# Cos-GLU behind an FFT filter: the first product of the last 18 token chunks by seven block products instead of eight, and the two small chunks moved forward

## The chip, the core and the metric

One NeuronCore of a Trainium2 chip runs the whole program. The metric is the device time of one execution in microseconds, lower is better. Before the change it is 2460.77 us, the median of three runs (2459.45 to 2461.38).

## What is computed

```python
batch, seq, dim = (8, 3008, 256)
X = np.fft.rfft(x, axis=1)
Y = X * (filt_r + 1j * filt_i)[None]
y = np.fft.irfft(Y, n=seq, axis=1)          # float32
x = y.reshape(24064, 256)                    # tokens
h = x @ w_in                                 # 256 x 2048
g = h * np.cos(h)
out = g @ w_out                              # 2048 x 256, float32
```

## The kernel before

**Staging.** The filter runs as a two-factor FFT (47 x 64) in four stages on TensorE, batch by batch, with intermediate results in DRAM. Its last step, `stage4` (L500 to L546), leaves the tokens of a chunk in SBUF as two rounded parts, `yh` (high) and `yl` (low remainder). The two dense products follow chunk by chunk: 50 chunks of 470 tokens (5 groups of 94) and, at the end, 2 of 282 (`_chunks`).

**A step.** A chunk has 8 steps `s`, each of 256 of the 2048 hidden columns. `hidden(c, s)` is the first product: for two halves `u` of 128 hidden columns and two halves `t` of the 256 inputs, three matmuls (weights high x tokens high, high x low, low x high), so 12 matmuls of 128x128 weights against 470 tokens into two PSUM banks `hp` (L561). `gate` (L569 to L584) then makes h*cos(h) from PSUM: a rounding on ACT (L571), a subtraction on DVE (L572), the sine on ACT (L575), a multiplication on DVE (L576), a rounded copy `gh` on ACT (L581) and the remainder `gl` on GpSimd (L582), each over 128x940. `project(c, s)` is the second product, 12 matmuls (L596) that add onto two banks `acc0`, `acc1`; after the eighth step ACT scales them (L605) and its queue sends them out.

**Order.** The program's PE order is written out: step k issues `hidden` of step k, then `project` of step k-2 (LAG). So a gate has the time of four blocks of 12 matmuls. Between the blocks `run_due` puts the pieces of the FFT of later batches by a list of due times, in slots, 64 to a chunk; `stage4` of a chunk stands there too. On ACT, DVE and GpSimd the order comes from the compiler's list of what is ready. In PSUM `ps_f` has 2 banks for the FFT, `ps_h` 4 (two `hp`), `ps_o` 2.

**Lines.** L528 is `stage4`'s matmul, L537 its copy on ACT, L538 and L539 its sums on DVE, L542 and L543 the split of its result; L261 to L263 are three matmuls of an FFT stage, L340 an FFT copy from PSUM on DVE, L380 an FFT product on DVE with one PSUM input, L639 and L642 a fill and a copy on GpSimd at the start.

Of the kernel before, what the change touches and what calls it, by code (L numbers as in the profile page):

```python
# [22 lines left out]
NJ = NB // 2  # L23
TJ = 2 * NA
# [138 lines left out]
def fft_filter_then_cos_glu(ctx: ExitStack, tc: tile.TileContext, ins, outT):  # L163
# [339 lines left out]
    def stage4(c, half):  # L503


        j0, n = chunks[c]
        r, w = n * NK, n * Q
        rows = z2.rearrange("j q d -> (j q) d")[j0 * 2 * Q + half * w :][:w]
        zf = fft.tile([P, 2, D], F32, name="z4", tag="ld", bufs=5)[:r]
        if c == 0:  # L510
            zf = zf[: 10 * (n23 - DIRECT)]
            of = z2c[2 * half : 2 * half + 2].rearrange("a g i (k d) -> (g i k) a d", k=2)
            load = nc.sync.dma_start(zf, of)
            hold[:] = [load.ins]
# [19 lines left out]
        y = fft.tile([P, NDT, 5, NA], F32, name="y4", bufs=1)[:, :, :n]  # L534
# [11 lines left out]
        done.add((c, half))  # L546


    gs, accs, first_gate = {}, {}, []

# [16 lines left out]
            gs[c, s] = gate(hp[:, :, :nt], nt, nc.vector if c == 0 else nc.gpsimd)  # L567

    def gate(h, nt, engine):  # L569
        g = moe.tile([P, 2, 5 * TJ], F32, name="g")[:, :, :nt]  # L570
# [8 lines left out]
        gh = moe.tile([P, 2, 5 * TJ], F32R, name="gh")[:, :, :nt]  # L579
        gl = moe.tile([P, 2, 5 * TJ], F32R, name="gl")[:, :, :nt]  # L580
        cast = nc.scalar.copy(gh, g)  # L581
        lower = engine.tensor_tensor(gl, g, gh.bitcast(F32), ALU.subtract)  # L582
        hold[1:] = [cast.ins, mult.ins, lower.ins]
        return gh, gl  # L584

    def project(c, s):
        nt = chunks[c][1] * TJ
        if s == 0:
            accs[c] = [ps_o.tile([P, 512], F32, name=f"acc{e}") for e in range(2)]
        gh, gl = gs.pop((c, s))  # L590
        for e in range(2):
            acc = accs[c][e][:, :nt]
            es = slice(e * P, (e + 1) * P)
            for u in range(2):
                for n, (w, g) in enumerate(((0, gh), (1, gh), (0, gl))):
                    nc.tensor.matmul(acc, w_out[s][w][:, u, es], g[:, u],  # L596
                                     start=(s == 0 and u == 0 and n == 0),
                                     stop=(s == NFT // 2 - 1 and u == 1 and n == 2))
                if e == 0 or u == 0:
                    yield  # L600
        if s == NFT // 2 - 1:
            t0 = chunks[c][0] * TJ
            for e in range(2):
                o = moe.tile([P, 5 * TJ], F32, name="o", bufs=2)[:, :nt]
                nc.scalar.activation(o, accs[c][e][:, :nt], AF.Copy, scale=TWO_PI)  # L605
                nc.scalar.dma_start(outT[e * P : (e + 1) * P, t0 : t0 + nt], o)
            del accs[c], ys[c]


    def pipeline(items, parts, gap=2):  # L610

# [81 lines left out]
    def convert(g=None, behind=None):  # L693
        with tc.issue_after((behind or hold)[1]), tc.issue_after((behind or hold)[2]):
            if g is None:
                g = prep.pop(0)(None)
                next(g)
            next(g, None)
# [59 lines left out]
    for c in range(1, len(chunks)):  # L758
        j0, n = chunks[c]
        each = EACH4 if c > 2 else 2 * SLOTS  # L760
        for half in range(2):
            at = [max(SLOTS * NS * c + (2 * half + t) * each - BEFORE4, SLOTS * (3 + 2 * half + t)) for t in range(NDT)]
            b = (2 * j0 + (half + 1) * n - 1) // NB
            plan(stage4(c, half), at[0] - AHEAD4, at, lambda b=b: len(wrote2.get(b, ())) == n23)
    due.sort(key=lambda d: d[0])
    for k in range(len(steps) + LAG):
        parts = []
        if k == 2:
            for g in soon[2:]:
# [75 lines left out]
```

## Time and profile before

| | us |
|---|---|
| median of 3 runs | 2460.77 |
| the profiled execution, device time | 2459.8 |
| its span, first to last instruction | 2457.7 |
| PE busy in the span | 2428.6 |
| GpSimd, ACT, DVE busy | 1606.9, 1616.3, 1442.9 |

The profile is of one execution. A busy PE is not a PE at its peak: a matmul's record runs past the start of the next, so the pace is read from starts (or from the chain, whose pieces don't overlap), not from the records' lengths. The span falls into three stretches: the first batch's FFT and filling up to some 70 us, the steps with the FFT of the other batches between them up to about 1640 us, and the steps alone after that.

### The profile page before, as it was taken

To read this page: it belongs to the slowest core of one execution; us is meant where nothing else is said; L and a number is where in the kernel's file an instruction comes from. 1 tells how busy PE (TensorE), PEld (TensorE's weight loads), DVE (VectorE), ACT (ScalarE), POOL (GpSimd) and SP (SyncE) were. 2 spreads that over 40 slices of the span, in tenths; PEclk is the share of its full clock that TensorE was granted. 3 is DMA by queue.
4 is the path that set the end of the run, shared out by engine and by line. 5 is a ranking of instruction groups with operands and counts; after the bars stand their busy time and mean duration, and the time that the engine had idled before them with its cause. 6 is when DMAs were issued, how large, how long until landed. Compare 5 with 4: busy or idle time off the path is not lost.

```text
span 2457.7 us, 32775 instructions
## 1 busy us (share of the span) xinstructions
PE 2428.6 (99%) x11671; PEld 2105.6 (86%) x11671; DVE 1442.9 (59%) x1814; ACT 1616.3 (66%) x2116; POOL 1606.9 (65%) x992
## 2 busy tenths in 40 slices
PE   7999999999999999999999999999999999999999
PEld 2788888888888888888888888888888888888888
DVE  5846756676676667567667766754444444444444
ACT  4866676677676767766776676666556565655665
POOL 3736677878787787878878887844444454444444
PEclk9999999999999999999999999999999999999999
DMA  8932354545554554454446444510000000000000
GB/s 293 270 115 89 107 147 130 178 137 162 150 157 131 148 177 150 131 174 151 142 134 190 148 137 136 165 62 21 28 17 32 17 29 20 21 25 13 17 8 18
DMA packets 185114, 268.98 MB, mean 109 GB/s; under 512 B 19089, under 2 KB 103249, under 8 KB 184953
## 3 DMA queue, kind: packets, MB, share of 16 engines
q1 hardware_dynamic: 151992, 214.72, 29.7%
q10 hardware_dynamic: 32960, 52.18, 5.9%
q8 instruction: 93, 1.52, 0.3%
q14 instruction: 69, 0.56, 0.1%
HBM read 172.96 MB, written 93.86 MB: 109 GB/s over the span
## 4 chain that ended last, share of the span: by engine, by line
PE 94%; DMA 2%; DVE 2%; issue 1%; ACT 1%; POOL 1%; SPq 0%; POOLq 0%; ACTq 0%; DVEq 0%
PE hp L561 42%; PE acc L596 41%; PE ps L528 3%; PE ps L338 2%; PE ps L261 2%; PE ps L262 2%; PE ps L263 2%; DMA ff<-in_fa 1%; PE hp L434 0%; PE ps L311 0%; DVE g L572 0%; DVE sw L379 0%; DVE g L576 0%; DMA raw<-in_w_out 0%; DMA ff<-in_fb 0%
## 5 line engine op out<-in xcount | busy, mean ns | idle before, releaser
L582 POOL TENSOR_TENSOR gl<-g,gh 128x940 fp32r<-128x940 f32 (+1 forms) x408 | 894.4, 2192 | 644.5 <-ACT gh L581 509.7
L561 PE MATMUL hp<-y,w_in 128*128 128x470 f32 (+1 forms) x4992 | 1154.0, 375 | 5.7 <-DVE g L576 5.3
L561 PEld LDWEIGHTS hp<-y,w_in 128*128 128x128 f32 x4992 | 929.5, 189 | 137.6 <-issue 5.9
L596 PE MATMUL acc<-gh,w_out 128*128 128x470 f32 (+1 forms) x3328 | 927.4, 374 | 0.8 <-ACT gh L581 0.5
L572 DVE TENSOR_TENSOR g<-g,hp 128x940 f32<-128x940 int32 (+1 forms) x416 | 464.4, 1116 | 425.6 <-ACT g L571 421.2
L596 PEld LDWEIGHTS acc<-gh,w_out 128*128 128x128 f32 x3328 | 618.7, 189 | 86.6 <-issue 1.5
L576 DVE TENSOR_TENSOR g<-g,hp 128x940 f32<-128x940 f32 (+1 forms) x416 | 464.6, 1117 | 349.4 <-ACT g L575 348.2
L575 ACT ACTIVATE g<-g,half_pi 128x940 f32<-128x940 f32 (+1 forms) x416 | 445.3, 1070 | 236.4 <-DVE g L572 230.0
L596 PE MATMUL acc<-gl,w_out 128*128 128x470 f32 (+1 forms) x1664 | 567.8, 375 | 1.4 <-POOL gl L582 1.4
L571 ACT ACTIVATE g<-hp 128x940 int32<-128x940 f32 (+1 forms) x416 | 391.7, 942 | 235.1 <-PE hp L561 225.5
L581 ACT CAST gh<-g 128x940 fp32r<-128x940 f32 (+1 forms) x416 | 400.6, 963 | 197.4 <-DVE g L576 191.7
L596 PEld LDWEIGHTS acc<-gl,w_out 128*128 128x128 f32 x1664 | 311.9, 188 | 44.7 <-POOL gl L582 2.2
L333 POOL TENSOR_TENSOR xh<-xf,xh 48x512 fp32r<-48x512 f32 x192 | 245.3, 1291 | 42.2 <-ACT xh L332 32.7
L379 DVE SCALAR_TENSOR_TENSOR sw<-ps,sg,f 64x256 f32<-64x256 f32 x336 | 162.4, 483 | 54.0 <-PE ps L263 48.8
L340 DVE COPY z1t<-ps 96x512 f32<-96x512 f32 x192 | 129.4, 684 | 98.6 <-PE ps L338 95.8
L543 POOL TENSOR_TENSOR y<-y,y 128x470 fp32r<-128x470 f32 (+1 forms) x100 | 114.7, 1147 | 48.1 <-ACT y L542 48.0
L332 ACT CAST xh<-xf 96x512 fp32r<-96x512 f32 x192 | 114.8, 618 | 34.3 <-PE ps L338 30.7
L385 POOL TENSOR_TENSOR yl<-ya,yh 128x512 fp32r<-128x512 f32 x84 | 109.0, 1299 | 34.7 <-ACT yh L384 34.2
L528 PEld LDWEIGHTS ps<-m,z 120*128 120x128 f32 (+1 forms) x816 | 114.5, 191 | 9.4 <-issue 0.8
L528 PE MATMUL ps<-m,z 120*128 120x120 f32 (+1 forms) x816 | 114.2, 273 | 0.1
L369 POOL TENSOR_TENSOR zl<-zf,zh 128x512 fp32r<-128x512 f32 x84 | 108.9, 1300 | 6.4 <-ACT zh L368 6.4
L364 POOL TENSOR_TENSOR zf<-zf,zg 128x512 f32<-128x512 f32 x72 | 93.6, 1300 | 13.2 <-DMA zg<-z 12.9
(96 smaller groups left out, 1196.4 us busy)
## 6 DMA issues: line engine op xcount, KB each, us to landing
xf<-in_x SPq DMA_DIRECT2D x224, 192.0 KB
z<-z1t SPq DMA_DIRECT2D x192, 192.0 KB
z<-z SPq DMA_DIRECT2D x98, 240.0 KB
out_t<-o ACTq DMA_DIRECT2D x100, 235.0 KB
f<-in_fb SPq DMA_DIRECT2D x84, 256.0 KB
f<-in_fa SPq DMA_DIRECT2D x84, 256.0 KB
zf<-z SPq DMA_DIRECT2D x84, 256.0 KB
z<-z2t ACTq DMA_DIRECT2D x84, 256.0 KB
```

Of the source, the lines that this page charges most:

```text
L333: nc.gpsimd.tensor_tensor(xh[:Q], xf[:Q, v], xh[:Q].bitcast(F32), ALU.subtract)
L340: nc.vector.tensor_copy(z, ps[: 2 * Q])
L379: nc.vector.scalar_tensor_tensor(sw[to, ks], ps[of, ks], sg[of, kc : kc + 1], fbt[of, ks], ALU.mult, ALU.mult)
L528: mm = nc.tensor.matmul(v[:, t, a * r : (a + 1) * r], zf[:, a, t * P : (t + 1) * P], m, start=c > 0, stop=c > 0 or a == 1)
L561: mm = nc.tensor.matmul(hp[:, u, :nt], w_in[s][w][:, t, fs], y[:, t, :nt], start=(t == 0 and n == 0), stop=(t == NDT - 1 and n == 2))
L571: rounded = nc.scalar.activation(g.bitcast(I32), h, AF.Copy, bias=0.25)
L572: rest = nc.vector.tensor_tensor(g, g.bitcast(I32), h, ALU.subtract)
L575: sine = nc.scalar.activation(g, g, AF.Sin, bias=half_pi, scale=-TWO_PI)
L576: mult = nc.vector.tensor_tensor(g, g, h, ALU.mult)
L581: cast = nc.scalar.copy(gh, g)
L582: lower = engine.tensor_tensor(gl, g, gh.bitcast(F32), ALU.subtract)
L596: nc.tensor.matmul(acc, w_out[s][w][:, u, es], g[:, u], start=(s == 0 and u == 0 and n == 0), stop=(s == NFT // 2 - 1 and u == 1 and n == 2))
```

## The change

The small chunks of 282 tokens become chunks 4 and 5, in place of the last two; the due times are counted in token groups. From chunk 34 (`FAST`) on, a chunk's first product goes by Winograd's form of Strassen's scheme. The operands of a 256-column step are taken as 2x2 blocks: the weights by `t` and `u`, the tokens by `t` and the two halves of the chunk (235 tokens, held as 236). Seven block products replace eight. Four sums of weight blocks (`add_weights`, S1 to S4) are made once, and four of token blocks (T1 to T4) for each chunk in `blocks`, on GpSimd, which takes the place of the end of `stage4`; each is split into a high part and a remainder.

A `quad` handles two steps at once: `product` issues 6 matmuls of 236 columns (3 for each of the two steps) for each of the seven products, 42 in all, into the four banks x (two in turn), v and w of the new pool `ps_q`, and into one bank of `ps_f` for y. Three banks are copied out on ACT between the products that add onto them, and three sums are made on DVE. `factor` does the first four operations of the gate on each of the four results (128x472); the rounded copy goes to GpSimd for two of them and to ACT for the other two, the remainders to GpSimd. `project_quad` is the second product, 24 matmuls a quad with 472 columns. PE's order is again written out: a quad's projection runs one and two quads later. The core of the diff:

```diff
+SMALL, FAST = 4, 34
+HALF = 236
+SUMS, EACH_SUM = 2010, 12
+AHEAD_FAST = (64, 60, 52, 48)
+AFTER_FAST = (3, 7, 11, 15, 19)
...
-    sizes = [5] * ((B * NJ - 6) // 5) + [3, 3]
+    sizes = [5] * SMALL + [3, 3] + [5] * ((B * NJ - 6) // 5 - SMALL)
...
-    ps_h = ctx.enter_context(tc.tile_pool(name="ps_h", bufs=2, space=bass.MemoryType.PSUM))
     ps_o = ctx.enter_context(tc.tile_pool(name="ps_o", bufs=1, space=bass.MemoryType.PSUM))
+    until = ctx.enter_context(ExitStack())
+    ps_h = until.enter_context(tc.tile_pool(name="ps_h", bufs=2, space=bass.MemoryType.PSUM))
...
+        if c >= FAST:
+            e = v.rearrange("p t (i g n) -> p t i g n", g=2, n=NK)
+            yield from blocks(c, half, e)
+            done.add((c, half))
+            return
...
+    def add_weights(s):
+
+        hi, lo = (w.bitcast(F32).rearrange("p t f -> p (t f)") for w in w_in[s])
+        whole = fft.tile([P, 512], F32, name="whole", tag="ld", bufs=5)
+        nc.vector.tensor_tensor(whole, hi, lo, ALU.add)
...
+        nc.vector.tensor_tensor(both[:, 0], a21, a22, ALU.add)
+        nc.vector.tensor_tensor(both[:, 2], a21, a11, ALU.subtract)
+        nc.vector.tensor_tensor(both[:, 1], both[:, 0], a11, ALU.subtract)
+        nc.vector.tensor_tensor(both[:, 3], a12, both[:, 1], ALU.subtract)
...
+        nc.scalar.copy(sums[s][0], both)
+        nc.gpsimd.tensor_tensor(sums[s][1], both, sums[s][0].bitcast(F32), ALU.subtract)
+        yield
...
+    def split(hi, lo, of, cast=nc.scalar.copy):
+        cast(hi, of)
+        nc.gpsimd.tensor_tensor(lo, of, hi.bitcast(F32), ALU.subtract)
...
+        hi, lo = ys[c][:2]
+        yield
+        if half == 0:
+            split(hi[:, :2], lo[:, :2], blk[:, 1:3], nc.vector.tensor_copy)
+            return
...
+        first = fft.tile([P, 2, HALF], F32, name="dif", tag="y4", bufs=1)
+        second = blk[:, :2]
+        for r in range(2):
+            nc.gpsimd.tensor_tensor(first[:, r], blk[:, 0], blk[:, 2 * r + 1], ALU.subtract)
+        yield
+        split(th[:, :2], tl[:, :2], first, nc.vector.tensor_copy)
+        yield
+        for r in range(2):
+            nc.gpsimd.tensor_tensor(second[:, r], blk[:, 1 + r], second[:, 0] if r else first[:, 1], ALU.subtract)
+        yield
+        split(th[:, 2:], tl[:, 2:], second, nc.vector.tensor_copy)
+        yield
+        split(hi[:, 2:], lo[:, 2:], blk[:, 3:], nc.vector.tensor_copy)
...
+    def factor(h):
+        g = wprep.tile([P, 512], F32, name="qg", tag="t", bufs=5)[:, : 2 * HALF]
+        nc.scalar.activation(g.bitcast(I32), h, AF.Copy, bias=0.25)
+        nc.vector.tensor_tensor(g, g.bitcast(I32), h, ALU.subtract)
+        nc.scalar.activation(g, g, AF.Sin, bias=half_pi, scale=-TWO_PI)
+        nc.vector.tensor_tensor(g, g, h, ALU.mult)
+        return g
...
+    def product(q, bank, weights, y, first=False, last=False):
+        for p in range(2):
+            s = 2 * q + p
+            if weights < 4:
+                ws = [sums[s][i][:, weights] for i in range(2)]
+            else:
+                t, u = divmod(weights - 4, 2)
+                ws = [w_in[s][i][:, t, u * P : (u + 1) * P] for i in range(2)]
+            for i, (a, b) in enumerate(((0, 0), (0, 1), (1, 0))):
+                nc.tensor.matmul(bank[:, p * HALF : (p + 1) * HALF], ws[a], y[b],
+                                 start=first and p == i == 0, stop=last and i == 2, skip_group_check=True)
...
+    def copy(bank):
+        to = fft.tile([P, 512], F32, name="sum", tag="st", bufs=4)[:, :N2]
+        with tc.high_priority():
+            nc.scalar.copy(to, bank)
+        return to
...
+    def begin(c, q):
+        k = NFT // 4 * (c - FAST) + q
+        x = ps_q.tile([P, 512], F32, name=f"x{k % 2}")[:, :N2]
+        product(q, x, A11, rows(c, B11), first=True)
+        nexts[c, q] = x, copy(x)
...
+        v, w = (ps_q.tile([P, 512], F32, name=name)[:, :N2] for name in "vw")
+        y = ps_f.tile([P, 512], F32, name="ps", tag="ps")[:, :N2]
+        block(x, S2, T2)
+        p16 = copy(x)
+        yield
+        block(y, A12, B21, first=True, last=True)
+        nc.vector.tensor_tensor(y, y, p1, ALU.add)
+        block(w, S3, T3, first=True)
+        p7 = copy(w)
+        gy = factor(y)
+        yield
+        h0, l0 = gate_tile(), gate_tile()
+        split(h0[:, 0], l0[:, 0], gy, nc.gpsimd.tensor_copy)
+        block(x, S1, T1)
+        with tc.high_priority():
+            nc.vector.tensor_tensor(v, x, p7, ALU.add)
+        block(w, A22, T4, last=True)
+        with tc.high_priority():
+            nc.vector.tensor_tensor(w, w, p16, ALU.add)
+            gw = factor(w)
+        after = (c, q + 1) if q + 1 < NFT // 4 else (c + 1, 0)
+        if after[0] < len(chunks):
+            begin(*after)
+        h1, l1 = gate_tile(), gate_tile()
+        gv = factor(v)
+        for a, g in ((0, gw), (1, gv)):
+            nc.scalar.copy(h1[:, a], g)
+            with tc.high_priority():
+                nc.gpsimd.tensor_tensor(l1[:, a], g, h1[:, a].bitcast(F32), ALU.subtract)
+        yield
+        yield
+        block(x, S4, B22, last=True)
+        gx = factor(x)
+        split(h0[:, 1], l0[:, 1], gx, nc.gpsimd.tensor_copy)
+        gs[c, q, 0], gs[c, q, 1] = (l0, h0), (l1, h1)
+    def project_quad(c, q, u):
...
+        order = [(p, e) for e in range(2) for p in range(2)]
+        for i, (p, e) in enumerate(order):
+            acc = accs[c][e][:, : 2 * HALF].rearrange("p (a n) -> p a n", a=2)
+            w = w_out[2 * q + p]
+            for n, (a, b) in enumerate(((0, h), (1, h), (0, g))):
+                nc.tensor.matmul(acc, w[a][:, u, e * P : (e + 1) * P], b[:, :, p],
+                                 start=(q, u, p, n) == (0, 1, 0, 0), stop=(end and p == 1 and n == 2))
+            if end and p == 1:
+                o = moe.tile([P, HALF * 2], F32, name="o", bufs=2)
+                with tc.high_priority():
+                    if e:
+                        nc.vector.tensor_scalar(o, accs[c][e][:, : 2 * HALF], TWO_PI, None, ALU.mult)
+                    else:
+                        nc.scalar.activation(o, accs[c][e][:, : 2 * HALF], AF.Copy, scale=TWO_PI)
+                t0, nt = chunks[c][0] * TJ, 5 * TJ
...
-        c = max(c for c in range(len(chunks)) if chunks[c][0] <= j)
-        return SLOTS * NS * (c + (j - chunks[c][0]) / chunks[c][1])
+        return SLOTS * NS * j / 5
...
+                at = [slot(j0) - a for a in AHEAD_FAST[2 * half : 2 * half + 2]]
...
+    until.close()
+    ps_q = ctx.enter_context(tc.tile_pool(name="ps_q", bufs=1, space=bass.MemoryType.PSUM, reuse_waits="tile"))
+    with tc.manual_schedule(engines={mybir.EngineType.PE}):
+        now = slot(chunks[FAST][0])
+        begin(FAST, 0)
+        for _ in range(SLOTS // 2):
+            next(old[0], None)
+        before = None
+        for k in range(len(quads) + 2):
+            if k < len(quads):
+                parts = quad(*quads[k])
+            else:
+                parts = iter(())
+            back = [project_quad(*quads[k - 2], 0)] * 2 if k > 1 else []
+            if 0 < k <= len(quads):
+                ready = [project_quad(*quads[k - 1], 1)] * 2
+            else:
+                ready = []
+            if k == 0:
+                order = [[old[1]]] * 4
+            elif k == 1:
+                order = [[old[2]] * 2] * 2 + [[g] for g in ready]
+            else:
+                order = [[g] for g in back + ready]
+            if before:
+                next(before, None)
+            for i in range(4):
+                run_due(now)
+                next(parts, None)
+                now += SLOTS // 4
+                run_due(now)
+                for g in order[i] if i < len(order) else ():
+                    next(g, None)
+                now += SLOTS // 4
+            before = parts
 
 
 # ---- launch: one core; the host lays data out ----
```

## Rows read from the trace of the kernel before

**Rows 1.** Page, part 1: busy us of each engine, share of the span, instructions.

```profile
PE 2428.6 (99%) x11671; PEld 2105.6 (86%) x11671; DVE 1442.9 (59%) x1814; ACT 1616.3 (66%) x2116; POOL 1606.9 (65%) x992
```

**Rows 2.** Stretches: length, busy PE, PEld, DVE, ACT, POOL (instructions), clock, DMA share, GB/s.

```profile
312.00:359.00 47.00, 47.00 (x228) 41.09 (x227) 26.58 (x32) 34.69 (x48) 38.40 (x25) 1.00 0.58 155
1517.00:1568.00 51.00, 50.56 (x242) 43.42 (x241) 35.28 (x52) 34.77 (x48) 48.01 (x33) 1.00 0.62 194
...
1711.00:2354.00 643.00, 643.00 (x3118) 568.77 (x3117) 290.21 (x301) 388.52 (x451) 300.40 (x151) 1.00 0.06 21
...
2400.00:2420.00 20.00, 20.00 (x145) 19.58 (x144) 8.39 (x12) 12.73 (x20) 9.76 (x7) 1.00 0.07 25
```

**Rows 3.** Chain of work that ended last, by time: start, us, what.

```profile
2304.44 2.58 PE acc L596 x12
2307.02 2.57 PE hp L561 x12
...
2315.57 0.85 PE ps L528 x8
...
2414.68 1.56 PE hp L561 x12
```

**Rows 4.** Timeline of PE: start, us, form and count; 256 columns, then 72 columns.

```profile
895.38 0.28 PE L262 MATMUL ps<-yh,m 128*128 128x256 f32 x1
...
895.86 0.28 PE L263 MATMUL ps<-yl,m 128*128 128x256 f32 x1
...
2315.58 0.50 PE L528 MATMUL ps<-m,z 72*128 72x72 f32 x3
...
2315.92 0.50 PE L528 MATMUL ps<-m,z 72*128 72x72 f32 x3
```

**Rows 5.** Groups by line and form, whole span: count, busy us, mean ns of one, idle before.

```profile
L571 ACT ACTIVATE g<-hp 128x940 int32<-128x940 f32 x400 | 381.4, 954 | 221.8 <-PE hp L561 212.2 <-POOL xh L333 5.8 <-DMA out_t<-o 1.6
L571 ACT ACTIVATE g<-hp 128x564 int32<-128x564 f32 x16 | 10.3, 642 | 13.3 <-PE hp L561 13.3
...
L575 ACT ACTIVATE g<-g,half_pi 128x940 f32<-128x940 f32 x400 | 433.0, 1083 | 232.6 <-DVE g L572 226.2 <-ACT o L605 4.2 <-DVE y L539 0.4
L575 ACT ACTIVATE g<-g,half_pi 128x564 f32<-128x564 f32 x16 | 12.3, 768 | 3.8 <-DVE g L572 3.8
...
L572 DVE TENSOR_TENSOR g<-g,hp 128x940 f32<-128x940 int32 x400 | 452.5, 1131 | 413.0 <-ACT g L571 408.8 <-POOL zl L369 0.7
L572 DVE TENSOR_TENSOR g<-g,hp 128x564 f32<-128x564 int32 x16 | 11.9, 742 | 12.6 <-ACT g L571 12.4
...
L542 ACT CAST y<-y 128x470 fp32r<-128x470 f32 x100 | 58.0, 580 | 8.0 <-DVE y L539 7.7
...
L605 ACT ACTIVATE o<-acc 128x470 f32<-128x470 f32 x100 | 53.7, 557 | 14.4 <-PE acc L596 13.9 <-DMA zf<-z 0.3
...
L380 DVE TENSOR_TENSOR ps<-ps,f 128x512 f32<-128x512 f32 x84 | 58.2, 693 | 0.6
...
L543 POOL TENSOR_TENSOR y<-y,y 128x470 fp32r<-128x470 f32 x96 | 111.6, 1162 | 45.3 <-ACT y L542 45.1
L543 POOL TENSOR_TENSOR y<-y,y 128x282 fp32r<-128x282 f32 x4 | 3.1, 780 | 2.8 <-ACT y L542 2.8
L582 POOL TENSOR_TENSOR gl<-g,gh 128x564 fp32r<-128x564 f32 x16 | 22.5, 1409 | 27.4 <-ACT gh L581 25.1 <-issue 2.3
...
L642 POOL COPY few<-f 128x20 f32<-128x20 f32 x2 | 0.3, 201 | 15.8 <-DMA f<-in_f 15.8
...
L537 ACT COPY odd<-ps 128x240 f32<-128x240 f32 x98 | 35.0, 358 | 15.8 <-PE ps L528 15.5
L538 DVE TENSOR_TENSOR y<-ps,odd 128x240 f32<-128x240 f32 x98 | 39.6, 404 | 33.8 <-POOL y L543 20.9 <-ACT odd L537 12.3
```

**Rows 6.** The chain's last pieces: start, us, what.

```profile
2446.00 1.58 PE hp L561 x12
2447.58 0.02 issue
...
2452.92 0.80 PE acc L596 x4
...
2454.63 0.41 ACT o L605
```

More of the change, by code (lines that the diff above doesn't have):

```diff
@@ L546, in stage4 @@
         done.add((c, half))
+    sums = {}
+    def add_weights(s):
+        hi, lo = (w.bitcast(F32).rearrange("p t f -> p (t f)") for w in w_in[s])
+        whole = fft.tile([P, 512], F32, name="whole", tag="ld", bufs=5)
+        nc.vector.tensor_tensor(whole, hi, lo, ALU.add)
+        (a11, a21), (a12, a22) = ((whole[:, 2 * t * P : (2 * t + 1) * P], whole[:, (2 * t + 1) * P : (2 * t + 2) * P]) for t in range(NDT))
+        both = fft.tile([P, 4, P], F32, name="both", tag="ld", bufs=5)
+        nc.vector.tensor_tensor(both[:, 0], a21, a22, ALU.add)
+        nc.vector.tensor_tensor(both[:, 2], a21, a11, ALU.subtract)
+        nc.vector.tensor_tensor(both[:, 1], both[:, 0], a11, ALU.subtract)
+        nc.vector.tensor_tensor(both[:, 3], a12, both[:, 1], ALU.subtract)
+        sums[s] = []
+        if s == NS - 1:
+            two = fft.tile([P, 2, 4, P], F32R, name="sum", tag="f", bufs=3)
+            sums[s].extend(two[:, i] for i in range(2))
+        else:
+            for tag, bufs in places[s]:
+                sums[s].append(fft.tile([P, 4, P], F32R, name="sum", tag=tag, bufs=bufs))
+        nc.scalar.copy(sums[s][0], both)
+        nc.gpsimd.tensor_tensor(sums[s][1], both, sums[s][0].bitcast(F32), ALU.subtract)
+        yield
@@ new lines, in fft_filter_then_cos_glu, with blocks @@
+    places = [(("sh", 3), ("sl", 3))] * 3 + [((tag, 2),) * 2 for tag in ("ya", "sw", "yl", "yh")]
+    blks, highs = {}, []
+    def split(hi, lo, of, cast=nc.scalar.copy):
+        cast(hi, of)
+        nc.gpsimd.tensor_tensor(lo, of, hi.bitcast(F32), ALU.subtract)
+    def blocks(c, half, e):
+        if half == 0:
+            blks[c] = wprep.tile([P, 4, 256], F32, name="blk", tag="raw", bufs=3).rearrange("p r n -> p (r n)")[:, : 4 * HALF].rearrange("p (r n) -> p r n", r=4)
+            nc.gpsimd.memset(blks[c][:, :, HALF - 1 :], 0.0)
+            ys[c] = [ypool.tile([P, NDT, 5 * TJ], F32R, name=f"y{i}").rearrange("p t n -> p (t n)")[:, : 3 * HALF].rearrange("p (r n) -> p r n", r=3)
+                     for i in range(2)]
+        blk = blks[c]
+        rows = blk[:, 0:4:3] if half else blk[:, 1:3]
+        y = rows[:, :, : 5 * NA].rearrange("p t (i n) -> p t i n", n=NA)
+        odd = fft.tile([P, NDT, 5, NK], F32, name="odd", bufs=1)
+        nc.scalar.copy(odd, e[:, :, :, 1])
+        nc.vector.tensor_tensor(y[:, :, :, :NK], e[:, :, :, 0], odd, ALU.add)
+        nc.vector.tensor_tensor(y[:, :, :, NK:], e[:, :, :, 0, 1:], odd[:, :, :, 1:], ALU.subtract)
+        hi, lo = ys[c][:2]
+        yield
+        if half == 0:
+            split(hi[:, :2], lo[:, :2], blk[:, 1:3], nc.vector.tensor_copy)
+            return
+        if not highs:
+            highs.extend(fft.tile([P, 4, 256], F32R, name="diff", tag="f", bufs=3) for i in range(2))
+        th, tl = (t.rearrange("p r n -> p (r n)")[:, : 4 * HALF].rearrange("p (r n) -> p r n", r=4)
+                  for t in (highs[c % 2], wprep.tile([P, 4, 256], F32R, name="diff", tag="raw", bufs=3)))
+        first = fft.tile([P, 2, HALF], F32, name="dif", tag="y4", bufs=1)
[11 more added lines that the diff above has]
+        split(hi[:, 2:], lo[:, 2:], blk[:, 3:], nc.vector.tensor_copy)
+        ys[c] += [th, tl]
+        del blks[c]
@@ L569, in gate @@
     def gate(h, nt, engine):
-        g = moe.tile([P, 2, 5 * TJ], F32, name="g")[:, :, :nt]
+        g = moe.tile([P, 2, HALF * 2], F32, name="g")[:, :, :nt]
         rounded = nc.scalar.activation(g.bitcast(I32), h, AF.Copy, bias=0.25)
@@ L578, in gate @@
             first_gate.append([None, sine.ins, mult.ins])
-        gh = moe.tile([P, 2, 5 * TJ], F32R, name="gh")[:, :, :nt]
-        gl = moe.tile([P, 2, 5 * TJ], F32R, name="gl")[:, :, :nt]
+        gh = moe.tile([P, 2, HALF * 2], F32R, name="gh")[:, :, :nt]
+        gl = moe.tile([P, 2, HALF * 2], F32R, name="gl")[:, :, :nt]
         cast = nc.scalar.copy(gh, g)
@@ L603, in project @@
             for e in range(2):
-                o = moe.tile([P, 5 * TJ], F32, name="o", bufs=2)[:, :nt]
+                o = moe.tile([P, HALF * 2], F32, name="o", bufs=2)[:, :nt]
                 nc.scalar.activation(o, accs[c][e][:, :nt], AF.Copy, scale=TWO_PI)
@@ L607, in project, with gate_tile @@
             del accs[c], ys[c]
+    turn = [0]
+    def gate_tile():
+        tag = ("g", "gh", "gl")[turn[0] % 3]
+        turn[0] += 1
+        return moe.tile([P, 2, HALF * 2], F32R, name="h" + tag, tag=tag)
+    def factor(h):
[5 more added lines that the diff above has]
+        return g
@@ new lines, in fft_filter_then_cos_glu @@
+    N2 = 2 * HALF
+    S1, S2, S3, S4, A11, A21, A12, A22 = range(8)
+    B11, B21, B22, T1, T3, T2, T4 = range(7)
+    nexts = {}
+    def product(q, bank, weights, y, first=False, last=False):
[9 more added lines that the diff above has]
+                                 start=first and p == i == 0, stop=last and i == 2, skip_group_check=True)
@@ new lines, in copy, with rows @@
+    def copy(bank):
[3 more added lines that the diff above has]
+        return to
+    def rows(c, r):
+        bh, bl, th, tl = ys[c]
+        return (bh[:, r], bl[:, r]) if r < 3 else (th[:, r - 3], tl[:, r - 3])
+    def begin(c, q):
[3 more added lines that the diff above has]
+        nexts[c, q] = x, copy(x)
@@ new lines, in quad, with block @@
+    def quad(c, q):
+        def block(bank, weights, r, **kw):
+            product(q, bank, weights, rows(c, r), **kw)
+        if (c, q) not in nexts:
+            begin(c, q)
+        x, p1 = nexts.pop((c, q))
+        v, w = (ps_q.tile([P, 512], F32, name=name)[:, :N2] for name in "vw")
[33 more added lines that the diff above has]
+        gs[c, q, 0], gs[c, q, 1] = (l0, h0), (l1, h1)
+        if q == NFT // 4 - 1:
+            del ys[c]
@@ new lines, in project_quad @@
+    def project_quad(c, q, u):
+        if (q, u) == (0, 1):
+            accs[c] = [ps_o.tile([P, 512], F32, name=f"acc{e}") for e in range(2)]
+        g, h = (t.rearrange("p a (s n) -> p a s n", s=2) for t in gs.pop((c, q, u)))
+        end = (q, u) == (NFT // 4 - 1, 0)
+        order = [(p, e) for e in range(2) for p in range(2)]
[13 more added lines that the diff above has]
+                t0, nt = chunks[c][0] * TJ, 5 * TJ
+                to = outT[e * P : (e + 1) * P, t0 : t0 + nt].rearrange("p (a n) -> p a n", a=2)
+                nc.scalar.dma_start(to, o.rearrange("p (a n) -> p a n", a=2)[:, :, : 5 * NA])
+            if i % 2:
+                yield
@@ L715, in fft_filter_then_cos_glu @@
         load_full("m40", "m41")
-    steps = [(c, s) for c in range(len(chunks)) for s in range(NS)]
+    steps = [(c, s) for c in range(FAST) for s in range(NS)]
     due = []
@@ L761, in fft_filter_then_cos_glu @@
         for half in range(2):
-            at = [max(SLOTS * NS * c + (2 * half + t) * each - BEFORE4, SLOTS * (3 + 2 * half + t)) for t in range(NDT)]
+            at = [max(slot(j0) + (2 * half + t) * each - BEFORE4, SLOTS * (3 + 2 * half + t)) for t in range(NDT)]
+            if c >= FAST:
+                at = [slot(j0) - a for a in AHEAD_FAST[2 * half : 2 * half + 2]]
             b = (2 * j0 + (half + 1) * n - 1) // NB
-            plan(stage4(c, half), at[0] - AHEAD4, at, lambda b=b: len(wrote2.get(b, ())) == n23)
+            plan(stage4(c, half), at[0] - AHEAD4, at, lambda b=B - 1 if c >= FAST else b: len(wrote2.get(b, ())) == n23)
+            if c >= FAST:
+                due.extend([at[1] + a, False, *due[-1][2:]] for a in AFTER_FAST[: 5 if half else 1])
+    for s in range(NS):
+        plan(add_weights(s), SUMS + EACH_SUM * s, [], lambda: len(wrote2.get(B - 1, ())) == n23)
     due.sort(key=lambda d: d[0])
-    for k in range(len(steps) + LAG):
+    left = []
+    for k in range(len(steps)):
         parts = []
@@ L773, in fft_filter_then_cos_glu @@
                 convert(g, tie)
+        c, s = steps[k]
         if k < len(steps):
-            c, s = steps[k]
             if s == 6 and c == 0:
@@ L784, in fft_filter_then_cos_glu @@
             parts.append(hidden(c, s))
-        if k >= LAG:
+        if k >= LAG and k < len(steps) - 1:
             parts.append(project(*steps[k - LAG]))
-        now = SLOTS * k
+        rate = chunks[c][1] / 5
+        now = slot(chunks[c][0]) + SLOTS * rate * s
         for g in parts:
@@ L791, in fft_filter_then_cos_glu @@
                 next(g, None)
-                now += 1
+                now += rate
+    quads = [(c, q) for c in range(FAST, len(chunks)) for q in range(NFT // 4)]
+    old = [project(*steps[k]) for k in range(len(steps) - LAG - 1, len(steps))]
+    until.close()
[20 more added lines that the diff above has]
+                order = [[old[2]] * 2] * 2 + [[g] for g in ready]
+            else:
+                order = [[g] for g in back + ready]
[10 more added lines that the diff above has]
+            before = parts
 def kernel(**inputs):
```

2 lines of the change are left out of this document (1 added, 1 removed).

## The prediction

> **What bounds the kernel now.** I read the page's busy times first, then the same by stretch, then the chain of work that ended last. PE is busy for 99% of the span, the other engines for 59 to 66% [rows 1]. In the stretch that the change rebuilds (15 whole chunks after the last FFT stage) PE has 643.00 of 643.00 us, ACT 60%, DVE 45%, GpSimd 47%, at clock 1.00 [rows 2]. The reader is to see that no other engine is near its limit there and that PE never waits: in the chain one block of 12 matmuls follows the next, 2.57 or 2.58 us each [rows 3]. So the time of this stretch is a count of matmuls times their spacing. The stretch holds 3118 matmuls, and 15 chunks of 16 blocks of 12 and 16 of `stage4` are 3120, so nothing else is in it; a chunk takes 643/15 = 42.87 us, a quad's worth (two steps) 10.72. The span is 2457.7 of the 2459.8 us of the profiled execution, which is 1.0 below the median. I sum against 2459.8 and add 1.0 at the end.
>
> **The product.** Spacing at 470 columns is 2.575/12 = 0.2146 us; at 282 columns 1.56/12 = 0.130 [rows 3]. A quad of before is 48 matmuls, 10.30 us, 5.15 for each product. The seven block products are 42 matmuls of 236 columns. What one of these takes isn't in the trace, and the whole change hangs on it: 24 x 0.2146 / 42 = 0.1226 us is break-even. From above, 256 columns with 128x128 weights of the same kind start 0.120 apart (four spacings from 895.38 to 895.86) [rows 4]. From below, the line through 470 and 282 columns gives 0.110 at 236. A third row tells of the weights: at 72 columns, with far less to stream, starts are still 0.113 apart (three spacings from 2315.58 to 2315.92; or three matmuls of some 0.275 within 0.50, 0.1125) [rows 4], and eight of them take 0.85 us [rows 3]. I read this as the time to load 128 columns of weights, hidden at 470 columns but a floor here. I take 0.1125, as the floor lies over the line; the ends are 0.110 and 0.120.
>
> So 42 x 0.1125 = 4.725 us replace 5.15. The second product keeps its 24 matmuls with 472 columns for 470, some 0.02 us more. Per quad -0.405 us; 18 chunks of 4 quads: **-29.2 us** (-36.8 at 0.110, -6.5 at 0.120). Seven for eight would be 12.5% of 5.15; the narrower matmul gives back a third of it.
>
> The Trainium skill, "TensorE: Matmul & The Clock Gate", section on LDWEIGHTS, has a weight load take its columns over 1.2 GHz, 107 ns for 128. By that, an estimate, the load would lie under the line above and the gain be that of the 0.110 end. The 72-column rows put the load a little higher, so I go by them.
>
> **The other engines.** At 472 wide I interpolate between 564 and 940 [rows 5]: rounding 0.642 - 92 x (0.954 - 0.642)/376 = 0.566, sine 0.691, each of the two DVE operations 0.647. A copy from PSUM on ACT is 0.557, a rounding cast 0.580, a DVE sum with a PSUM input 0.65 (0.693 at 512), a GpSimd remainder 1.165 [rows 5].
> - ACT per quad: 3 copies 1.67, 4 roundings and 4 sines 5.03, 2 casts 1.16: 7.86. Per chunk two `odd` copies and one output, 1.27, so 0.32 a quad: 8.18.
> - DVE: 8 x 0.647 and 3 sums, 7.13. Per chunk four sums of 0.40 (1.6), casts of 3.5 x 472 elements at most at the PSUM price (2.2) and one output (0.65), 1.1 a quad: 8.24.
> - GpSimd: 4 remainders 4.66 and 2 casts. Only a copy of 20 columns is shown, 0.201 [rows 5]; between that and a remainder's 1.165 I take 0.6, since a copy reads one tensor instead of two: 5.86. Per chunk four differences of 236 (0.68 each, 282 take 0.78) and 3.5 remainders, 6.8, so 1.7 a quad: 7.57 (6.8 to 8.7).
>
> The new quad on PE is 10.72 - 0.405 = 10.32 us, so ACT is to be busy 79%, DVE 80%, GpSimd 73% (66 to 84%). The highest that a stretch shows is ACT 34.69/47 = 74%, DVE 35.28/51 = 69%, GpSimd 48.01/51 = 94% [rows 2], PE at 99% or more. They fit by sum, with less room than before.
>
> **The waits that are added.** PE's order is fixed, so a product that waits for a copy or a bank holds all of PE behind it. With blocks of 0.675 (products) and 1.29 us (six projections) I lay out a quad. The three tightest: (1) The first product of the next quad takes the x bank of the quad before; between that one's last product (S4) and this lie five products (S2, A12, S3, S1, A22), 3.37, and two half projections, 2.58: 5.95 us, against 2.55 for the four gate operations that must have read the bank. (2) The product with A22 adds onto w after ACT has copied w out: 1.29 + 0.675 = 1.96 us for a copy of 0.56 that may find ACT in an operation of 0.69. (3) The gates of v and w have from 5.95 us to the projection one quad later, 10.5 us, against a chain of 0.65 + 2.55 + 0.58 + 1.17 = 4.95, twice side by side. All have room for one foreign operation at each hop. Where GpSimd was fullest, PE lost 0.44 of 51 us to waits of this kind [rows 2]. I charge 0.1 us a quad, **+7 us** (0 to 0.2, 0 to 14; more is a rival below).
>
> **Ahead, between and behind.** `add_weights` (8 x 5 DVE sums, an ACT cast, a GpSimd remainder) and the first token sums fall behind the last FFT stage, due over 84 slots, 56 us at 64 slots to 42.87 us, in which DVE is 55% free; none of the 40 sums is wider than 512, so they take under 40 x 0.693 = 28 us. They cost nothing, a few us if they come late, which the next term's dear end takes in. At the change of pools the `hp` banks must be free: the first product needs the gate of a step that ended two blocks earlier or, if the banks lie the other way, of the last (four operations, 4.3 us at 940 wide). **+1 us** (0 to 4.5).
>
> The small chunks cost the same matmuls wherever they stand. At the end they ran with PE full [rows 2]. Early, they share GpSimd with the FFT: four blocks of 1.565 are 6.26 us; their gate takes 0.642 + 0.742 + 0.768 + 0.742, about 0.70 for the cast and 1.409 = 5.0 [rows 5]. One remainder of 1.16 in front fits, two don't, and cost 1 us. **+2 us** (0 to 8, half of 16 steps). The due times count groups now and so keep their place in the work; nothing for that.
>
> **The tail.** After the last product of before PE waits from 2447.58 to 2452.92, 5.3 us, and the output follows [rows 6]. Now 24 matmuls of other projections, 5.2 us, stand between the last product and the 12 that need its gate, 2.55 + 0.6 + 1.17 = 4.3; perhaps 1 us goes to the gates of v and w before it. The outputs go out by ACT and DVE side by side, the sum of their times about as before. **-4.5 us** (-5.3 to -3.5).
>
> **Sum.** -29.2 + 7 + 1 + 2 - 4.5 = -23.7: 2436 of 2459.8, **2437 us** beside the median. Its own range is 2418 (0.110, no waits) to 2456 (all else at its dear end, or 0.120 with half the waits).
>
> **Rivals.**
> (A) **ACT and DVE can't be filled to 80%.** The place is the alternation of ACT and DVE in four gates at once, on queues whose order is fixed before the run; an instruction that waits holds the ready ones behind it. For it: ACT never shows more than 74% and DVE 69%, and an ACT rounding has 221.8/400 = 0.55 us of idle time before it [rows 2, 5]. Against: more independent chains are open now, and GpSimd reached 94%. It decides when DVE stays under 8.24/10.72 = 77%. At 74% the quad takes 11.14 us, 72 x 0.42 = +30, with the tail and the rest 2489; at 69%, 2540. Slower. Chance 0.22.
> (B) **The gain turns into one wait**, (1) or (2) above, of some 0.4 us a quad: two foreign operations at each of four hops of the x gate are 2.55 + 8 x 0.6 = 7.4 us against 5.95, one each 5.0, so the average case is near the edge. PE saves 29 and waits 29, only the tail is left: 2456 to 2464. Chance 0.12.
> (C) **Loads are full at 282 columns already.** There PEld is busy 19.58 of 20.00 us, at 470 columns 88% [rows 2]. If a load took 0.130 us, 42 would be 5.46: 72 x 0.33 = +24, 2482. The 256- and 72-column rows speak plainly against it [rows 4]: the load records overlap. Chance 0.03.
> A rule of the Trainium skill leads to (C): its first page, "Trainium Kernel Development and Optimization", Performance Expectations, has the busy share of LDWEIGHTS as the good measure of a kernel's distance from its limit. Here it says that nothing narrower can pay; the spacings say otherwise, and they are measured.
>
> **How the numbers follow.** Forecast 0.63, A 0.22, B 0.12, C 0.03. 0.2%, about 5 us, is what a measurement of this kernel can tell from no change. The forecast's range is all but 0.03 of it faster by more; B is mostly within, a little on either side; A and C are slower. Faster 0.63, same 0.10, slower 0.27. The range runs from 2416 up into A, where about 0.15 is left above 2484.
>
> **What would show it.** In the changed trace: products of 236 columns 0.1125 apart, six in 0.675 us, and a chunk in 41.3 instead of 42.87 us from chunk 34 on. Under A, PE's waits are spread over several lines with ACT or DVE as releasers and the quad is over 10.72; under B they sit at one or two of the products, by the same amount in every quad; under C products are 0.13 apart with no wait. Before 1640 us the two traces should differ by under 10 us. GpSimd casts of over 1.2 us, or a transition that leaves PE idle for more than 5 us, would make the forecast wrong by terms that I took as small.

## The result and the profile after

The changed kernel takes 2439.6 us (median of 4 runs, 2437.42 to 2439.80) against 2460.11 for the kernel before (4 runs); the ratio is 0.9915, 95% interval 0.9897 to 0.9932. So it is some 20.5 us faster (17 to 25 by the interval), where the prediction said 2437 and -23.7. The profiled execution is the fastest of the four, 2437.42 us with a span of 2435.6.

Two stretches answer to [rows 2]: the change-over, and 16 whole chunks of block products (columns as there).

```profile
1600.00:1690.00 90.00, 80.09 (x394) 68.65 (x393) 68.62 (x93) 52.81 (x70) 56.31 (x37) 1.00 0.14 43
...
1723.60:2383.20 659.60, 659.60 (x4482) 618.29 (x4481) 490.98 (x848) 471.87 (x882) 485.93 (x528) 1.00 0.07 23
```

In the second PE is again full. A chunk takes 659.6/16 = 41.23 us against 42.87, 1.64 less, and DVE, ACT and GpSimd are busy 74, 72 and 74%. In the first PE stands idle for 9.9 of 90 us; in the kernel before it was 0.8 in the same 90 us:

```profile
1600.00:1690.00 90.00, 89.24 (x445) 78.65 (x444) 46.92 (x60) 54.68 (x70) 44.72 (x25) 1.00 0.15 51
```

The chain in a quad of the steady stretch (start, us, what):

```profile
1964.54 0.67 PE w L720 x6
1965.21 1.29 PE acc L796 x6
1966.50 0.67 PE x L720 x6
1967.17 0.68 PE w L720 x6
1967.84 0.67 PE x L720 x6
1968.51 2.57 PE acc L796 x12
```

Six products of 236 columns take 0.67 us, 0.112 each, where [rows 4] gave 0.113 for 72 columns and 0.120 for 256. Nothing stands between the blocks. Who PE waited for says the same, first in the change-over, then from 1690 us to the end (us in total, times, longest):

```profile
PE hp L642 <- DVE g L657: 3.5, 2, 2.4
PE x L720 <- ACT sum L726: 2.5, 1, 2.5
PE ps L267 <- DVE ya L387: 1.3, 1, 1.3
...
PE acc L796 <- POOL hgl L775: 0.6, 1, 0.6
```

The last line is the only wait from 1690 us to the end of the span, 746 us; it is in the tail.

By terms, measured in the two traces: 18 chunks x 1.64 = -29.6; the change-over +9.1; the tail about nothing. That is -20.5 in all, the difference of the medians. The two profiled executions lie 22.4 us apart (2459.8 and 2437.42), and the 2 us between are put to no term.

### The profile page after: what moved, and what is told of

Its sections match the earlier page's. It is cut to its first block, busy times and chain, and to the rows that moved or that the text cites. A ratio compares the mean times of both kernels' runs of the same rounds, so it can differ in the third digit from the quotient of the medians.

```text
span 2435.6 us, 37066 instructions
## 1 busy us (share of the span) xinstructions
PE 2396.6 (98%) x12967; PEld 2117.1 (87%) x12967; DVE 1675.9 (69%) x2448; ACT 1684.6 (69%) x2574; POOL 1805.8 (74%) x1414
## 4 chain that ended last, share of the span: by engine, by line
PE 92%; DVE 4%; DMA 2%; ACT 1%; issue 1%; SPq 0%; POOL 0%; ACTq 0%; DVEq 0%; POOLq 0%
PE hp L642 26%; PE acc L677 26%; PE acc L796 15%; PE x L720 8%; PE w L720 4%; PE ps L534 3%; PE ps L720 2%; PE ps L344 2%; PE ps L267 1%; PE ps L268 1%; PE ps L269 1%; DVE sw L385 1%; DVE g L653 1%; DVE g L657 1%; DMA ff<-in_fa 1%
## 5 line engine op out<-in xcount | busy, mean ns | idle before, releaser
L663 POOL TENSOR_TENSOR gl<-g,gh 128x940 fp32r<-128x940 f32 (+1 forms) x264 | 575.4, 2180 | 270.2 <-ACT gh L662 164.1
L642 PE MATMUL hp<-y,w_in 128*128 128x470 f32 (+1 forms) x3264 | 753.2, 373 | 9.4 <-DVE g L657 8.7
L642 PEld LDWEIGHTS hp<-y,w_in 128*128 128x128 f32 x3264 | 605.0, 189 | 97.5 <-issue 11.7
L677 PE MATMUL acc<-gh,w_out 128*128 128x470 f32 (+1 forms) x2176 | 607.1, 372 | 0.0
L677 PEld LDWEIGHTS acc<-gh,w_out 128*128 128x128 f32 x2176 | 404.2, 189 | 57.4 <-issue 1.7
L677 PE MATMUL acc<-gl,w_out 128*128 128x470 f32 (+1 forms) x1088 | 372.4, 375 | 0.5 <-POOL gl L663 0.4
L702 ACT ACTIVATE qg<-qg,half_pi 128x472 f32<-128x472 f32 x288 | 192.0, 690 | 70.6 <-DVE qg L701 70.6
L796 PE MATMUL acc<-hgl,w_out 128*128 128x472 f32 x576 | 186.6, 378 | 0.6 <-POOL hgl L775 0.6
L796 PE MATMUL acc<-hg,w_out 128*128 128x472 f32 x576 | 186.7, 378 | 0.0
L796 PE MATMUL acc<-hgh,w_out 128*128 128x472 f32 x576 | 186.6, 378 | 0.0
```

The costliest lines, as they stand in the source:

```text
L642: mm = nc.tensor.matmul(hp[:, u, :nt], w_in[s][w][:, t, fs], y[:, t, :nt], start=(t == 0 and n == 0), stop=(t == NDT - 1 and n == 2))
L677: nc.tensor.matmul(acc, w_out[s][w][:, u, es], g[:, u], start=(s == 0 and u == 0 and n == 0), stop=(s == NFT // 2 - 1 and u == 1 and n == 2))
L796: nc.tensor.matmul(acc, w[a][:, u, e * P : (e + 1) * P], b[:, :, p], start=(q, u, p, n) == (0, 1, 0, 0), stop=(end and p == 1 and n == 2))
```

## Experiments

With the result known, the theory had three parts. (F) A product's spacing is the load of its 128 weight columns. (S) The loss at the change-over is the weight sums of `add_weights` on DVE. (R) The other engines have room. Each has its rival below. The expectations take the loss at the change-over as 11 us; by PE's busy time it is 9.1.

**Small chunks alone.** On the kernel before: `sizes = [5] * 4 + [3, 3] + [5] * ...`, and the due times counted in groups.

> The kernel before with only the small chunks moved forward and the due times counted in groups; no block products. The prediction charged +2 us for this (0 to 8). In the trace of the changed kernel PE loses only some 0.5 us between 250 and 400 us, where the small chunks now are. Theory: the move costs nothing, 2459 to 2462. Rival: the small chunks' gates crowd GpSimd beside the FFT and the end of the program loses what they hid, 2463 to 2468.

Measured 2458.91 us (10 runs) against 2459.36, ratio 0.9997 (0.9988 to 1.0007). That is 0.45 us less, with an interval from 3.0 less to 1.7 more: no cost is seen.

**Weight sums on GpSimd.**

```diff
-        nc.vector.tensor_tensor(whole, hi, lo, ALU.add)
+        nc.gpsimd.tensor_tensor(whole, hi, lo, ALU.add)
...
-        nc.vector.tensor_tensor(both[:, 0], a21, a22, ALU.add)
+        nc.gpsimd.tensor_tensor(both[:, 0], a21, a22, ALU.add)
```

and so for the other three.

> The changed kernel with the five weight sums of each step (add_weights) on GpSimd instead of DVE. In the changed kernel PE loses some 11 us more than before between 1600 and 1690 us. Theory S: that is the 40 weight sums on DVE, which stand in front of the gates' operations, and of which several took 1.2 to 2.3 us instead of 0.28 beside a GpSimd instruction. Then 2431 to 2435, and PE waits for DVE nearly gone before 1655 us. Rival P: the loss belongs to the change of pools and the first quad (the copy of its first product on ACT came late, 2.5 us) and to the end of the FFT; then 2438 to 2441, or more if GpSimd is now in the way.

Measured 2429.61 us (4 runs), ratio to before 0.9882 (0.9865 to 0.9898): 10.0 us under the changed kernel by the medians, 7.7 by the profiled executions (2429.74 and 2437.42), more than expected. The change-over, and who PE waited for in it:

```profile
1600.00:1690.00 90.00, 87.66 (x461) 77.94 (x460) 54.51 (x73) 59.08 (x82) 77.41 (x74) 1.00 0.14 45
...
PE hp L642 <- DVE g L657: 1.7, 1, 1.7
PE x L720 <- ACT sum L726: 0.7, 1, 0.7
```

PE's idle time falls from 9.9 to 2.3 us, although GpSimd is now busy for 77.41 of the 90 us. Theory S holds for 5.7 us of this. The other 1.8 are the wait for the late copy of the first new product (L726), 0.7 for 2.5, and the traces put them elsewhere. In the changed kernel the copy stands on ACT behind the last rounding of the old gates:

```profile
1684.47 0.98 ACT L662 CAST gh<-g 128x940 fp32r<-128x940 f32 x1 [1.20 <-DVE g L657]
1685.35 0.55 ACT L726 COPY sum<-x 128x472 f32<-128x472 f32 x1
...
1685.95 0.93 PE L720 MATMUL x<-diff,sum 128*128 128x236 f32 x6 [2.53 <-ACT sum L726]
```

It stands there in this run too, but here eight matmuls of a projection, 1.7 us, lie in PE's order between the old gate's product and the first new one, and none in the changed kernel. So some 2.5 us of the loss belong to the change of pools, as rival P had it.

**Block products from chunk 43 only.** `FAST = 43`, `SUMS = 2586`.

> The changed kernel with block products in the last 9 chunks only (from chunk 43), and the weight sums as far ahead of them as before, now long after the last FFT stage. Gain per chunk by the traces 42.87 - 41.22 = 1.65 us, so 14.9 us from 9 chunks. Theory S (the loss at the transition comes from weight sums that meet the end of the FFT): the transition costs 3 to 5 us here, 2448 to 2451. Rival P (it belongs to the change of pools and the first quad, wherever it stands): 11 us again, 2455 to 2458.

Measured 2448.88 us (4 runs), ratio 0.9959 (0.9944 to 0.9974), 10.5 under before. Nine chunks give 14.8, so by the medians the change-over costs some 4.3 us when no FFT stage ends beside it. In the trace PE stands idle for 5.95 us there, against 9.9 at chunk 34, and waits for two things:

```profile
1870.00:2075.00 205.00, 199.05 (x971) 175.01 (x970) 119.00 (x133) 123.50 (x147) 109.31 (x62) 1.00 0.06 20
...
PE hp L642 <- DVE g L657: 3.4, 4, 1.7
PE x L720 <- ACT sum L726: 2.5, 1, 2.5
```

So some 4 us of the loss come with the place. The 40 sums took 31 us here too, and the late copy is as late as at chunk 34.

**The casts of GpSimd on ACT.** `split(h0[...], l0[...], gy, nc.scalar.copy)`, and the same for `gx`.

> The changed kernel with the two rounded copies that GpSimd makes in each quad (0.60 us each) on ACT (0.58 each). ACT goes from 71.5% busy in the steady stretch to some 83%, GpSimd from 74 to 62%. Theory: PE's spacing alone sets the quad and ACT has room; 2438 to 2442, the chunk stays at 41.2 us with no PE waits. Rival A of the prediction (ACT and DVE can't be filled to 80%): PE waits appear in every quad, the chunk goes to 42 us or more, 2450 to 2490.

Measured 2440.55 us (4 runs), ratio 0.9925 (0.9911 to 0.9940). The same 16 chunks:

```profile
1725.30:2384.90 659.60, 659.60 (x4482) 618.17 (x4481) 511.78 (x849) 526.48 (x1009) 418.61 (x399) 1.00 0.07 23
```

ACT is busy 79.8% and DVE 77.6%, the chunk is unchanged and PE has no wait in the loop. Theory R holds up to 80% of ACT; rival A of the prediction falls with it.

**Narrower corrections.**

```diff
-                nc.tensor.matmul(bank[:, p * HALF : (p + 1) * HALF], ws[a], y[b],
+                n = HALF if i == 0 else HALF // 2
+                nc.tensor.matmul(bank[:, p * HALF : p * HALF + n], ws[a], y[b][:, :n],
```

> The changed kernel with two of the three matmuls of each product (the corrections, high x low and low x high) cut from 236 to 118 columns; 28 of 42 a quad. It leaves these corrections out for half of the tokens, the number of matmuls and weight loads stays. Theory F (the spacing of 0.112 us is the load of 128 weight columns, a floor at 236 columns): the spacing stays at 0.112 and the time at 2437 to 2442. Rival (the columns still set the spacing, as the line through 470 and 282 columns has it): 118 columns take some 0.06 us, the quad needs 28 x 0.05 = 1.4 us less on PE, and the time falls by up to 100 us, to 2340 to 2370, unless another engine stops it on the way.

Measured 2441.87 us (4 runs), ratio 0.9928 (0.9912 to 0.9945). A third of the product's columns is gone and the chunk still takes 41.2 us. In its chain the groups of six, now one of 236 and two of 118 columns twice over, take:

```profile
1804.26 1.34 PE acc L797 x6
1805.60 0.61 PE x L721 x6
1806.22 0.67 PE w L721 x6
1806.89 0.67 PE x L721 x6
1807.56 2.63 PE acc L797 x12
1810.19 0.61 PE x L721 x6
```

The 0.06 that some groups lack stands at the projection in front (1.34 for 1.29, 2.63 for 2.57). Single spacings within a triple are uneven (medians 0.166 after the 236 columns, 0.057 between the two of 118, 0.111 to the next), but three matmuls take 0.334, 0.1113 each, wherever no projection stands in front. The weight loads (PEld) of the same matmuls begin evenly, here for four matmuls that start at 2002.31, 2002.47, 2002.53 and 2002.64:

```profile
2002.25 0.19 PEld L721 LDWEIGHTS w<-diff,w_in 128*128 128x128 f32 x1
2002.36 0.19 PEld L721 LDWEIGHTS w<-diff,w_in 128*128 128x128 f32 x1
2002.48 0.19 PEld L721 LDWEIGHTS w<-diff,w_in 128*128 128x128 f32 x1
2002.59 0.19 PEld L721 LDWEIGHTS w<-diff,w_in 128*128 128x128 f32 x1
```

Theory F holds as far as this goes: the columns are not what a product costs here, and its weight loads come 0.112 apart, while starts of matmuls can lie 0.057 apart. That it is the 128 weight columns which take this time is not shown: no narrow matmul of this case loads fewer. No other engine holds PE back: DVE is busy 491.68 of 659 us, as before this edit.

**A DVE sum measured by itself.** Two sums of 128x128 are added in each quad, one with two SBUF inputs (L768), one with a PSUM input (L769):

```diff
+        nc.vector.tensor_tensor(probe[:, 0], p1[:, :P], p7[:, :P], ALU.add)
+        nc.vector.tensor_tensor(probe[:, 1], v[:, :P], p7[:, :P], ALU.add)
```

> The changed kernel with two extra sums of 128x128 on DVE in each quad, results unused: one with both inputs in SBUF, one with the first input in PSUM. GpSimd is busy 74% of the stretch. Theory S (a DVE instruction with both inputs in SBUF doesn't start while a GpSimd instruction runs, and ends some 0.15 us after it): the SBUF sum takes 0.28 us with GpSimd idle, up to 1.3 beside it, 0.6 to 0.9 in the mean, and the PSUM sum stays at 0.25 to 0.3 throughout. Rival (those sums were long for another reason, such as the engine's own order or the small size): both alike. The time itself should move by under 3 us, as DVE has room; by 5 us or more if the held sums push the gates behind them late.

Measured 2439.29 us (2 runs). The groups (count, busy us, mean ns):

```profile
L768 DVE TENSOR_TENSOR probe<-sum 128x128 f32<-128x128 f32 x72 | 40.0, 555 | 2.1 <-ACT sum L727 0.6
L769 DVE TENSOR_TENSOR probe<-v,sum 128x128 f32<-128x128 f32 x72 | 20.4, 284 | 0.0
```

The same size costs 555 ns with two SBUF inputs and 284 with one. Matching starts against GpSimd's instructions: 18 of the first kind began with GpSimd idle and took 285 ns; 54 lay beside one and took 645 in the mean, ending some 148 ns after it. Of the second kind 18 began beside one and took 280. The time did not move as far as two runs tell, and PE has no wait in the loop: a held sum costs nothing here, where DVE has room.

**The same sums with one input in PSUM.** The sum of the two weight parts goes to a bank of `ps_f`, ACT copies it, and each block sum reads one input from the bank.

```diff
+        bank = ps_f.tile([P, 512], F32, name="ps", tag="ps")
+        nc.vector.tensor_tensor(bank, hi, lo, ALU.add)
...
+        nc.scalar.copy(whole, bank)
...
-        nc.vector.tensor_tensor(both[:, 0], a21, a22, ALU.add)
+        nc.vector.tensor_tensor(both[:, 0], b21, a22, ALU.add)
```

> The changed kernel with the sum of a step's two weight parts written to a PSUM bank, so that the four block sums on DVE each read one input from PSUM and one from SBUF; one copy of 512 on ACT is added per step. All 40 sums stay on DVE. With them on GpSimd the time was 2429.6. Theory H (of the loss at the transition the larger part is DVE held beside GpSimd): the 32 block sums take 0.28 us each, PE loses some 5 us less there, 2431 to 2435. Rival L (the loss is the DVE work as such, held or not): 2437 to 2441.

Measured 2431.88 us (4 runs), ratio 0.9887 (0.9870 to 0.9903), 7.7 under the changed kernel. The sums, and PE's waits in the change-over:

```profile
L572 DVE TENSOR_TENSOR both<-ps,whole 128x128 f32<-128x128 f32 x8 | 2.3, 283 | 0.0
L575 DVE TENSOR_TENSOR both<-ps,both 128x128 f32<-128x128 f32 x8 | 2.3, 282 | 0.0
...
PE x L723 <- ACT sum L729: 2.8, 1, 2.8
PE acc L680 <- POOL gl L666: 0.7, 1, 0.7
```

In the changed kernel the four lines of these sums had means of 654 to 784 ns and took 24 us together; here they take 9, and PE's idle time in the 90 us falls from 9.9 to 3.6 us with all 40 sums still on DVE. So rival L does not hold, and DVE standing still has a large share in the loss. How large is not shown, for the edit also put the sums later: the first begins at 1627.3 us, 4 us before the last FFT matmul ends, where in the changed kernel six of the eight groups begin ahead of that end. The place alone took some 4 us off at chunk 43. What is left here over the run with the sums on GpSimd, 2.3 us, is within the intervals of the two; the late copy on ACT (2.8 against 0.7) would account for it. To put that copy earlier was not tried.

So two versions beat both kernels: 2429.6 us with the sums on GpSimd, 2431.9 with one input in PSUM.

## Why the prediction came out as it did

The time was right within 3 us, and its largest term was right. Several others were wrong and partly cancelled.

**The product: right.** The step read 72, 256, 282 and 470 columns together and took the floor of 0.1125 over the line's 0.110. Measured 0.112, and the narrow run bears out the reason as far as it goes: the floor is there without the columns, and the loads keep its pace. The chunk was to take 41.3 us and took 41.23; the term was -29.2 and came to -29.6. Rival C (loads full at 0.130) falls with it. PEld is busy 618.29 of 659.60 us, 94%, in a loop where the loads set the pace of 42 matmuls of a quad's 66, and was at 98% at 282 columns, where the columns set it (0.130). So the busy share alone doesn't tell which of the two binds; the page of the Trainium skill behind rival C ("Trainium Kernel Development and Optimization", Performance Expectations) would have led astray here.

**The other engines: right, a little dear.** Forecast 79, 80 and 73% for ACT, DVE and GpSimd; measured 72, 74 and 74%. The sums added single durations. ACT's durations in the 16 chunks do add up to 524.8 us, 79.6%, but instructions that follow each other at once overlap by some 0.1 us, 52.9 in all, so ACT and DVE are less busy than the sum. So the sign given for rival A, DVE under 77%, came with PE full and decides nothing. The GpSimd cast, bounded between 0.2 and 1.165 and taken as 0.6, is 0.60.

**The added waits: the step failed, in size.** +7 us was charged; there is none in the loop. The x bank has room to spare, and so has the copy of w on ACT, which is the closer of the two:

```profile
2002.26 0.84 PE L720 MATMUL x<-y,sum 128*128 128x236 f32 x6
...
2005.79 0.65 DVE L703 TENSOR_TENSOR qg<-qg,x 128x472 f32<-128x472 f32 x1 [1.35 <-ACT qg L702]
...
2006.48 0.56 ACT L726 COPY sum<-w 128x472 f32<-128x472 f32 x1 [0.72 <-PE w L720]
...
2008.20 0.83 PE L720 MATMUL w<-diff,w_in 128*128 128x236 f32 x6
2008.88 0.84 PE L720 MATMUL x<-y,w_in 128*128 128x236 f32 x6
```

The last read of the bank ends at 2006.44, the product that takes it begins at 2008.88, 2.4 us later (1.6 at the least in the whole loop). The copy of w ends at 2007.04, 1.16 us before the product that adds onto w (0.56 at the least). The gate of x took 3.5 us for 2.55 by sum, one foreign operation or two on the way and not at each hop. Rival B falls.

**The change-over: the step failed.** The prediction set `add_weights` at nothing, since at most 28 us of DVE sums would fit into a stretch where DVE is 55% free, and gave +1 us (to 4.5) for the banks. It cost 9; more than 5 us of idle PE was one of its own signs of being wrong. Three things were missed. Most of the sums didn't fall behind the FFT: DVE took them between the last FFT stage's own operations and the gates, from 1578.6 to 1647.7 us, in front of work that PE waited for. Their price was bounded by the duration of an instruction with one input in PSUM. And ACT's copy of the first new product stood behind the last old gate, 2.5 us. In the trace after, DVE (first) and GpSimd stand like this:

```profile
1643.44 1.06 DVE L569 TENSOR_TENSOR both<-whole 128x128 f32<-128x128 f32 x1
1644.43 2.28 DVE L570 TENSOR_TENSOR both<-whole 128x128 f32<-128x128 f32 x1
1646.63 0.38 DVE L604 TENSOR_TENSOR blk<-ps,odd 128x230 f32<-128x230 f32 x1
...
1641.37 2.98 POOL L581 TENSOR_TENSOR sum<-both,sum 128x512 fp32r<-128x512 f32 x2 [3.70 <-ACT sum L580]
1644.31 2.25 POOL L663 TENSOR_TENSOR gl<-g,gh 128x940 fp32r<-128x940 f32 x1
```

GpSimd's instructions end at 1644.35 and 1646.56; the DVE sums, begun while they ran, end at 1644.50 and 1646.71, 0.15 after each. The 40 sums took 32.5 us, over the bound of 28, for 14.5 undisturbed. At the change of pools no bank held PE up: the first new product began without a wait, and the 2.5 us came at the next one.

**The small chunks: too dear.** +2 charged, no cost seen when moved by themselves.

**The tail: the step failed in its reading.** [rows 6] was read as 5.3 us of idle PE. The chain there follows the last gate; it doesn't say that PE stood still. PE's own timeline of the kernel before shows it at work on other projections, with two gaps of 0.74 and 0.66:

```profile
2448.95 0.74 PE L596 MATMUL acc<-gh,w_out 128*128 128x282 f32 x4
2450.43 0.40 PE L596 MATMUL acc<-gl,w_out 128*128 128x282 f32 x1 [0.74 <-POOL gl L582]
...
2451.59 0.67 PE L596 MATMUL acc<-gh,w_out 128*128 128x282 f32 x4
2452.92 0.40 PE L596 MATMUL acc<-gl,w_out 128*128 128x282 f32 x1 [0.66 <-POOL gl L582]
```

After, there is one gap of 0.62, and the span now ends 4.2 us after the last matmul instead of 3.4, with both outputs issued by ACT's queue. The term was -4.5 and came to about nothing: 0.8 less in gaps, 0.8 more at the end.

So the misses are -0.4 (product), -7 (waits) and -2 (small chunks) against +8.1 (change-over) and +4.5 (tail): 9.4 us on one side, 12.6 on the other. The total owes its closeness to this, and that is luck.

## What to carry to other kernels

When fewer but narrower matmuls are the idea, price them by the narrowest matmuls in the trace as well as by a line through the wide ones: below some width columns no longer set the spacing (here 0.112 us a matmul, with 128 columns of weights), and columns cut beyond it buy nothing. One-time preparation that falls into the seam between two phases is not free because an engine is half idle there; ask which instructions stand behind it in that engine's queue. Read idle time from the engine's own timeline and not from the chain, which may follow another engine while this one works.

## What was not expected of the hardware

A DVE sum with two SBUF inputs that begins while a GpSimd instruction runs ended some 0.15 us after that one, up to 2.28 us for a sum that takes 0.28; with one input in PSUM it took 0.28 in either case (555 and 284 ns in the mean of 72 each). The Trainium skill, "GPSIMD Engine Reference", Specifications, names the interfaces that GpSimd shares with VectorE and contention with DVE instructions of two SBUF inputs; the runs agree and show that here it is a full stop until the GpSimd instruction has ended, and not a slower pace. The gates escape it: their DVE operations at 128x940, each with one input in PSUM, took 1.14 us at the most. Two inputs are not the whole condition: a cast of 128x472 with one SBUF input took 0.40 us with GpSimd idle and 0.88 in the median of the 18 (L588, `diff<-dif`) that began beside a GpSimd subtraction, ending some 0.26 us after that one.

Three matmuls of 236, 118 and 118 columns took 0.334 us, as three of 236 do, though the two narrow ones start only 0.057 apart. The loads begin evenly, 0.112 apart, and set the mean; why the starts are uneven is open.
